# Column norms of three batches: squares summed in fp32 on the vector engine, norms from N=1 matmuls, down projection one step later

## The chip, the cores and the metric

The kernel runs on one core of a Trainium2 chip. A core has a matrix engine (TensorE, PE in the profile, with its weight loads as PEld), a vector engine (VectorE, DVE), a scalar engine (ScalarE, ACT), GpSimd (POOL) and SyncE (SP); the last two issue transfers here. The metric is the device time of one execution in microseconds. The kernel before takes 527.6 us, the median of 3 runs (527.09 to 528.2).

## The reference

Two layers follow each other, over 4 batches of 6208 rows and 256 columns, all in float32. The first is a cross-covariance attention: q and k are normalized **by column**, so each of their 256 columns needs the sum of its squares over all 6208 rows.

```python
qn = q / (np.linalg.norm(q, axis=1, keepdims=True) + 1e-06)
kn = k / (np.linalg.norm(k, axis=1, keepdims=True) + 1e-06)
s = kn.transpose(0, 2, 1) @ qn / tau          # 256 x 256 per batch
a = softmax(s, -1)
x = v @ a
```

The second is a channel mix with a gate (d_model 256, d_ff 1024), on x and x shifted by one row:

```python
xk = mu_k * x + (1.0 - mu_k) * x_prev
xr = mu_r * x + (1.0 - mu_r) * x_prev
k = np.maximum(xk @ w_k, 0.0)
out = sigmoid(xr @ w_r) * (k * k @ w_v)
```

## The kernel before

**Two kinds of work, interleaved.** The rows of a batch are cut in 12 blocks of 512 rows and a rest of 64 (`NB` is 12, `NBLK` is 49: 48 blocks and one more that takes the four rests). The second layer runs over the blocks. The covariance of batch b+1 has to be ready when the second layer comes to batch b+1; so batch 0's covariance is computed first, by itself, and those of batches 1 to 3 are computed in small pieces between the matmuls of the second layer.

**Covariance in groups and units.** A batch of q and k is loaded in 13 groups: one of 64 rows, and 12 that give each of the 128 partitions four rows. For batches 1 to 3 GpSimd loads and casts to bf16 (`group_load`, L106). A *unit* is one row per partition. Per unit the kernel issues two matmuls into `s_ps` (`unit_matmul`, L138, the matmul is L149), and per two units one square on ScalarE into `qk2` (`unit_square`, L130, the square is L136).

**Norms.** When a group's four units are through, `group_norms` (L158) adds its squares into `ssq_ps`: four matmuls with a 128x32 block of ones as weights and 512 squares as the moving operand, each in its own 32 columns of the array (L166). At the batch's end ScalarE copies `ssq_ps` out (L193), VectorE copies `s_ps` (L229), and `gather` turns the sums into a column per partition with four fp32 matmuls of one column (L202; the profile shows two passes of each). Batch 0 does the same for its first groups, and for its last ones goes another way (`norms_direct`, L172): the squares are the weights, a single column of ones is the moving operand, N=1, and the sum lands in `bank` directly (L179).

**Softmax in pieces.** `softmax_pieces` (L182) returns 16 short steps for batches 1 to 3: root, inverse, spreading the norms over columns, scaling, exponential, weighing. One is taken from the list `chain` at each step of the loop.

**The loop sets the order.** The schedule is manual: each engine executes what the program issues in the order in which it is written. The outer loop (L574) runs i from -2 to 47, the inner j from 0 to 7. At step (i, j) the program issues

- `finish` (L431) at even j: on ScalarE a tanh of the gate (L436), on VectorE `res` (L437), the product with the down projection. `vr_ps`, which both read, has two buffers;
- a piece of `chain`;
- `up(i+1, j)` (L392): two matmuls into `kT_ps` (L398, three buffers) and a Relu on ScalarE (L402); `square` of the step before on VectorE (L408);
- `down(i, j)` (L411): for even j the gate's two matmuls (L423) and three of the down projection (L427), for odd j the other five;
- for block i+2: at j = 0 and 2 `x_half` (L315: two matmuls, L327, and a copy on ScalarE, L329), at j = 3 to 5 and 7 `mix_delta` and `mix` (L373, L383) on VectorE, and at j = 1 a last `mix` for block i+1;
- a unit where j is in `slots`: six steps of eight for blocks 2 to 7, three to five for the next three, four for the others.

## Time and profile before

| | |
|---|---|
| median of 3 runs | 527.6 us |
| the profiled execution | 527.0 us |
| its span, first to last instruction | 525.2 us |
| busy: PE, DVE, ACT | 507.9, 404.6, 425.9 us |
| granted TensorE clock, mean | 0.999 |
| instructions | 10152 |

The span is what the profile covers; the execution's time has some 1.8 us around it. A line of the timeline gives the start and the length in us, then engine, line, operation, output and inputs with the program's names, and a count where like instructions are merged; in brackets stands idle time before it and what ended it. Matmuls are pipelined, so a line's length is longer than the time until the next can start; what a matmul costs is read from start to start. A line of the groups gives busy time and the mean length in ns, then idle time ahead of the group and what ended most of it. A row of the stretches gives start and end, the length, the busy time of PE, PEld, DVE, ACT and POOL with counts, the granted clock, the share of the DMA engines and GB/s.

### The profile page before, as it was taken

What the parts mean: (1) busy time and instruction counts of PE and PEld (TensorE: products, weight loads), DVE (VectorE), ACT (ScalarE), POOL (GpSimd) and SP (SyncE); (2) the same over time, 40 slices, a digit from 0 to 9 for tenths busy, and PEclk for the clock granted to TensorE, in tenths of its full rate; (3) what the DMA queues carried; (4) which work ended last, traced back from release to release, by engine and by line L of the source; (5) the groups of instructions that cost most, each with busy time, mean ns of one, the idle gap of its engine ahead of it and who ended that gap; (6) DMA issues with size and microseconds to landing.
All of it is one profiled execution on the core that took longest, in us unless ns stands there. A gap on an engine that the chain in (4) does not pass through costs nothing.

```text
span 525.2 us, 10152 instructions
## 1 busy us (share of the span) xinstructions
PE 507.9 (97%) x3656; PEld 335.4 (64%) x3656; DVE 404.6 (77%) x959; ACT 425.9 (81%) x814; POOL 101.9 (19%) x143
## 2 busy tenths in 40 slices
PE   4878999999999999999999999999999999999996
PEld 2454566666666666666666666666666666666665
DVE  4558766776788787777777877777889989898984
ACT  6885988889888888888878888878878777778774
POOL 0055142322332221211143131210030101000000
PEclk9999999999999999999999999999999999999999
DMA  8999999999999999989899999995278575424113
GB/s 329 420 287 194 178 179 211 199 150 175 167 190 171 145 181 160 164 120 150 133 158 199 152 148 188 153 143 118 61 125 141 102 158 111 115 76 105 59 64 100
DMA packets 143738, 83.76 MB, mean 159 GB/s; under 512 B 51716, under 2 KB 140104, under 8 KB 143688
## 3 DMA queue, kind: packets, MB, share of 16 engines
q0 software_dynamic: 65808, 33.01, 54.1%
q1 hardware_dynamic: 77712, 49.98, 40.9%
q8 instruction: 28, 0.46, 0.4%
q14 instruction: 22, 0.18, 0.1%
q10 hardware_dynamic: 168, 0.13, 0.1%
HBM read 78.71 MB, written 25.43 MB: 198 GB/s over the span
## 4 chain that ended last, share of the span: by engine, by line
PE 90%; DMA 5%; DVE 2%; ACT 1%; SPq 1%; issue 0%; DVEq 0%; ACTq 0%
PE kT_ps L398 32%; PE vr_ps L427 32%; PE vr_ps L423 8%; PE xT_ps L327 8%; PE s_ps L149 6%; PE ssq_ps L166 2%; DMA f_385<-in_k_dram 2%; DMA f_261<-in_k_dram 2%; DMA f_165<-in_k_dram 1%; SPq L115 1%; DVE xk L383 1%; PE bank L202 0%; PE bank L226 0%; PE y_ps L464 0%; ACT L209 0%
## 5 line engine op out<-in xcount | busy, mean ns | idle before, releaser
L402 ACT ACTIVATE kr<-kT_ps 128x512 bf16<-128x512 f32 (+1 forms) x392 | 230.5, 599 | 58.4 <-PE kT_ps L398 46.1
L398 PE MATMUL kT_ps<-xk,w_k_sb 128*128 128x512 bf16 (+1 forms) x784 | 231.4, 377 | 0.3 <-DVE xk L383 0.2
L427 PE MATMUL vr_ps<-w_v_sb,kk 128*128 128x256 bf16 x1536 | 230.5, 273 | 0.0
L427 PEld LDWEIGHTS <-kk 128*128 128x128 bf16 x1536 | 150.3, 98 | 58.0
L408 DVE TENSOR_TENSOR kk<-kr 128x512 bf16<-128x512 bf16 (+1 forms) x392 | 155.7, 417 | 4.8 <-ACT kr L402 4.1
L437 DVE SCALAR_TENSOR_TENSOR res<-res,vr_ps 128x256 f32<-128x256 f32 x192 | 80.5, 419 | 81.9 <-ACT res L436 79.6
L398 PEld LDWEIGHTS <-w_k_sb 128*128 128x128 bf16 x784 | 73.2, 98 | 36.1 <-DVE kk L408 4.8
L149 PE MATMUL s_ps<-qk 128*128 128x256 bf16 (+1 forms) x392 | 71.6, 282 | 6.1 <-DVE qk L126 6.1
L436 ACT ACTIVATE res<-vr_ps 128x256 f32<-128x256 f32 x192 | 74.7, 389 | 0.5
L329 ACT CAST xT<-xT_ps 128x512 bf16<-128x512 f32 x94 | 55.9, 594 | 22.9 <-PE xT_ps L327 22.8
L423 PE MATMUL vr_ps<-w_r_sb,xr 128*128 128x256 bf16 x384 | 73.3, 273 | 0.6 <-DVE xr L383 0.6
L383 DVE SCALAR_TENSOR_TENSOR xr<-delta,mu_t,xT 128x512 bf16<-128x512 bf16 x96 | 71.7, 747 | 0.0
L383 DVE SCALAR_TENSOR_TENSOR xk<-delta,mu_t,xT 128x512 bf16<-128x512 bf16 x96 | 71.6, 747 | 0.0
L423 PEld LDWEIGHTS <-xr 128*128 128x128 bf16 x384 | 37.5, 98 | 45.4 <-DVE xr L383 1.1
L120 POOL DMA_DIRECT2D qk<-in_q_dram x39 | 28.7, 737 | 183.2 <-ACT res L436 151.2
L327 PE MATMUL xT_ps<-vT,a_sb 128*128 128x512 bf16 x188 | 55.9, 379 | 0.0
L290 POOL DMA_DIRECT2D v_bf<-in_v_dram x48 | 37.1, 774 | 67.4 <-DMA vT<-v_bf 62.1
L149 PEld LDWEIGHTS <-qk 128*128 128x128 bf16 (+1 forms) x392 | 37.9, 101 | 18.0 <-DVE qk L126 9.0
L373 DVE TENSOR_TENSOR delta<-xT 128x1024 bf16<-128x1024 bf16 x48 | 33.1, 690 | 9.5 <-ACT xT L329 9.4
L120 POOL DMA_DIRECT2D qk<-in_k_dram x39 | 28.3, 726 | 2.8 <-DMA w_v_sb<-in_moe_w_v_dram 1.6
L327 PEld LDWEIGHTS <-a_sb 128*128 128x128 bf16 x188 | 18.4, 98 | 2.9 <-issue 0.6
L214 POOL TENSOR_TENSOR rn<-rn,half 128x4 f32<-128x4 f32 x3 | 3.1, 1036 | 55.4 <-DVE rn L211 55.4
(225 smaller groups left out, 234.6 us busy)
## 6 DMA issues: line engine op xcount, KB each, us to landing
out_dram<-res SPq DMA_DIRECT2D x47, 512.0 KB, 5.0
v_bf<-in_v_dram POOLq DMA_DIRECT2D x48, 256.0 KB, 9.2
qk<-in_q_dram POOLq DMA_DIRECT2D x36, 256.0 KB, 6.0
qk<-in_k_dram POOLq DMA_DIRECT2D x36, 256.0 KB, 8.1
vT<-v_bf SPq DMA_TRANSPOSE x45, 8.5
f_104<-in_q_dram SPq DMA_DIRECT2D x1, 512.0 KB, 3.4
f_106<-in_k_dram SPq DMA_DIRECT2D x1, 512.0 KB, 4.1
f_128<-in_q_dram SPq DMA_DIRECT2D x1, 512.0 KB, 5.4
```

Source lines behind the costliest of these rows:

```text
L120: nc.gpsimd.dma_start(qk[:rows, :n, i, :], qk_src(t, b, g))
L149: nc.tensor.matmul(s_ps[:, ih, :], qk[:rows, s, 1, ih * P:(ih + 1) * P], qk[:rows, s, 0, :], start=t0 and ih == 0, stop=te, skip_group_che ...
L327: nc.tensor.matmul(xT_ps, a_sb[:, b, ih, dh * P:(dh + 1) * P], vT[:, :, ih, :], start=ih == 0, stop=ih == 1)
L329: nc.scalar.copy(xT[:, dh, 1:], xT_ps)
L383: nc.vector.scalar_tensor_tensor(o[:, dh], st[i, "d"][:, dh], mu[:, dh:dh + 1], st[i, "x"][:, dh, :M], op0=OP.mult, op1=OP.add)
L398: nc.tensor.matmul(kT_ps[:, :m], w_k_sb[:, dh, fh * P:(fh + 1) * P], xk[:, dh, :m], start=dh == 0, stop=dh == 1)
L402: nc.scalar.activation(kr[:, :m], kT_ps[:, :m], AF.Relu, scale=0.5 ** 0.5)
L408: nc.vector.tensor_tensor(st[i, "kk"][:, fh, :m], kr[:, :m], kr[:, :m], op=OP.mult)
L423: nc.tensor.matmul(vr_ps[:, D:], xr[:, dh, s * P:(s + 1) * P], w_r_sb[:, dh, :], start=dh == 0, stop=dh == 1)
L427: nc.tensor.matmul(vr_ps[:, :D], kk[:, fh, s * P:(s + 1) * P], w_v_sb[:, fh, :], start=fh == 0, stop=fh == 7)
L436: nc.scalar.activation(res[:, s], vr_ps[:, D:], AF.Tanh, scale=0.5)
L437: nc.vector.scalar_tensor_tensor(res[:, s], res[:, s], 1.0, vr_ps[:, :D], op0=OP.add, op1=OP.mult)
```

## The change

For batches 1 to 3:

- a unit's square is written in fp32 instead of bf16, into `sq2`, in the space of batch 0's fp32 loads;
- VectorE adds up a group's four rows of squares: `first` adds rows 0 and 1 to rows 2 and 3 (128x1024), `second` the two halves of that (128x512), with bf16 out;
- `group_norms_at` takes that sum as weights: four matmuls of N=1 into `bank`, in place of the four of N=512 and the later gather. A group of one row per partition goes without additions;
- the additions are issued at steps j = 7, 0 and 1 (at a batch's end also at others, two at a time), the norms some steps later. The softmax pieces wait at the root until the batch's norms have been issued;
- the copy of `s_ps` goes to ScalarE, and the copy of `ssq_ps` is gone.

For the second layer, in all batches: `down(i, j)` is issued at step j+1 (the last of a block at the next block's step 0), `finish` at odd steps instead of even ones, and both halves of `xr` are mixed in the block before their use, at j = 0 and 2.

```diff
@@ unit_square
-            nc.scalar.activation(qk2[:rows, s:e], qk[:rows, s:e], AF.Square)
+            if n == 1:
+                t = pq.tile([P, 1, 2 * C], BF16, name="sq", tag="sq1", bufs=1)
+            else:
+                t = pq.tile([P, 2, 2 * C], F32, name="sq2", tag=f"f{s // 2}", bufs=6)
+            groups[b, g] += (t,)
+            nc.scalar.activation(t[:rows], groups[b, g][0][:rows, s:e].rearrange("p s i c -> p s (i c)"), AF.Square)
+            if e == n:
+                adds.extend((now[0] + 2, b, g, f) for f in (group_adds(b, g) if n == S else []))
+                norms.append((b, g))
+                ready[b, g] = now[0] + 2
+
+    def group_adds(b, g):
+        sq2 = groups[b, g][1:]
+        sq = pq.tile([P, 1, 2 * C], BF16, name="sq", tag="sq", bufs=4)
+        def first():
+            nc.vector.tensor_tensor(sq2[0], sq2[0], sq2[1], op=OP.add)
+            groups[b, g] = (groups[b, g][0], sq)
+        def second():
+            nc.vector.tensor_tensor(sq, sq2[0][:, 0:1], sq2[0][:, 1:2], op=OP.add)
+        return [first, second]
+
+    def group_norms_at(b, g):
+        rows, n = rows_of(b, g)
+        t = groups[b, g][1]
+        if b not in bank:
+            bank[b] = ps.tile([P, 2 * C], F32, name="bank", tag="ssq_ps")
+        for u in range(1 if n == 1 else 1):
+            for i in range(4):
+                nc.tensor.matmul(bank[b][:, C + i:C + i + 1], t[:rows, u, i * P:(i + 1) * P], ones[:rows, 0:1],
+                                 start=g == 0 and i == 0, stop=g == NB, skip_group_check=True)
...
@@ softmax_pieces
-            (nc.vector.tensor_copy if b else nc.scalar.copy)(s_sb, s_ps)
+            nc.scalar.copy(s_sb, s_ps)
...
-        return [both, None, gather, roots, roots2, None, invert, None, None, spread, None, scale,
+        return [evac, None, None, roots, roots2, None, invert, None, None, spread, None, scale,
                 None if bounded else top, exp, None, weigh]
...
@@ last_block
+        down(i - 1, 7)
...
@@ the loop
-            if j % 2 == 0:
-                if j == 0 and i >= 1:
+            if j % 2:
+                if j == 1 and i >= 1:
                     finish(i - 1, 3)
-                elif j > 0 and i >= 0:
+                elif j > 1 and i >= 0:
                     finish(i, j // 2 - 1)
...
-                piece = chain.pop(0)
+                piece = chain[0]
+                if len(chain) == ROOTS and any(e[0] == holds[0] for e in norms):
+                    piece = None
+                else:
+                    chain.pop(0)
...
-            if i >= 0:
-                down(i, j)
+            if j > 0 and i >= 0:
+                down(i, j - 1)
+            elif j == 0 and i >= 1:
+                down(i - 1, 7)
...
-                if j == 7 and n != 1:
-                    mix(n, "xr", 0)
-            if j == 1 and 0 <= i + 1 < NBLK:
-                mix(i + 1, "xr", 1)
-            if i == 0 and j == 6:
-                mix(1, "xr", 0)
+
+            if j in (0, 2) and 0 <= i + 1 < NBLK:
+                mix(i + 1, "xr", int(j > 0))
...
+            if adds and adds[0][0] <= now[0] and (j in (0, 1, 7) or adds[0][1] == holds[0] and chain and j in (1, 5, 7)):
+                for _ in range(2):
+                    _, *e, f = adds.pop(0)
+                    f()
+                    ready[tuple(e)] = now[0] + 2
+                    if not (adds and adds[0][1] == holds[0] and chain):
+                        break
+
+            if norms and ready[norms[0]] <= now[0] and not any(e[1:3] == norms[0] for e in adds) and (
+                    norms[0][0] == holds[0] or len(chain) < 4):
+                group_norms_at(*norms.pop(0))
+            now[0] += 1
```

The order of the instructions at three places. First PE in the steady stage, around one group's norms. Before, they follow the last unit of their own group (L149):

```order
L149 LDWEIGHTS qk
L149 MATMUL s_ps<-qk 128x256
L166 LDWEIGHTS ones
L166 MATMUL ssq_ps<-qk_2524,ones 32x512
L166 LDWEIGHTS ones
L166 MATMUL ssq_ps<-qk_2524,ones 32x512
L166 LDWEIGHTS ones
L166 MATMUL ssq_ps<-qk_2524,ones 32x512
L166 LDWEIGHTS ones
L166 MATMUL ssq_ps<-qk_2524,ones 32x512
L398 LDWEIGHTS w_k_sb
L398 MATMUL kT_ps<-xk,w_k_sb 128x512
```

Now (L355 is the old L327, L426 the old L398):

```order
L355 LDWEIGHTS a_sb
L355 MATMUL xT_ps<-vT,a_sb 128x512
L173 LDWEIGHTS sq
L173 MATMUL bank<-ones,sq 128x1
L173 LDWEIGHTS sq
L173 MATMUL bank<-ones,sq 128x1
L173 LDWEIGHTS sq
L173 MATMUL bank<-ones,sq 128x1
L173 LDWEIGHTS sq
L173 MATMUL bank<-ones,sq 128x1
L426 LDWEIGHTS w_k_sb
L426 MATMUL kT_ps<-xk,w_k_sb 128x512
```

The norms stand at the end of step j = 2, behind x_half, and wait for VectorE's `second`, issued two steps before. Second, DVE in the steady stage, from one `res` to the next but one. Before:

```order
L437 SCALAR_TENSOR_TENSOR res<-res,vr_ps 128x256
L408 TENSOR_TENSOR kk<-kr 128x512
L322 COPY xT<-xT 128x2
L408 TENSOR_TENSOR kk<-kr 128x512
L383 SCALAR_TENSOR_TENSOR xr<-delta,mu_t,xT 128x512
L437 SCALAR_TENSOR_TENSOR res<-res,vr_ps 128x256
```

Now, in steps j = 7 and 0 (L465 is the old L437, L436 the old L408, L411 the old L383):

```order
L465 SCALAR_TENSOR_TENSOR res<-res,vr_ps 128x256
L436 TENSOR_TENSOR kk<-kr 128x512
L158 TENSOR_TENSOR sq_3392<-sq_3392,sq_3465 128x1024
L436 TENSOR_TENSOR kk<-kr 128x512
L350 COPY xT<-xT 128x2
L411 SCALAR_TENSOR_TENSOR xr<-delta,mu_t,xT 128x512
L162 TENSOR_TENSOR sq<-sq_3392 128x512
L465 SCALAR_TENSOR_TENSOR res<-res,vr_ps 128x256
```

Both additions of a group stand between two `res`. Third, DVE at the end of batch 1 (steps j = 7 of block 7 and j = 0 of block 8), where the copy of `s_ps` stood before:

```order
L437 SCALAR_TENSOR_TENSOR res<-res,vr_ps 128x256
L229 COPY s_sb<-s_ps 128x512
L408 TENSOR_TENSOR kk<-kr 128x512
L322 COPY xT<-xT 128x2
L408 TENSOR_TENSOR kk<-kr 128x512
L383 SCALAR_TENSOR_TENSOR xr<-delta,mu_t,xT 128x512
L437 SCALAR_TENSOR_TENSOR res<-res,vr_ps 128x256
```

Now:

```order
L465 SCALAR_TENSOR_TENSOR res<-res,vr_ps 128x256
L436 TENSOR_TENSOR kk<-kr 128x512
L158 TENSOR_TENSOR sq_1677<-sq_1677,sq_1721 128x1024
L162 TENSOR_TENSOR sq<-sq_1677 128x512
L436 TENSOR_TENSOR kk<-kr 128x512
L350 COPY xT<-xT 128x2
L411 SCALAR_TENSOR_TENSOR xr<-delta,mu_t,xT 128x512
L158 TENSOR_TENSOR sq_1792<-sq_1792,sq_1840 128x1024
L162 TENSOR_TENSOR sq<-sq_1792 128x512
L465 SCALAR_TENSOR_TENSOR res<-res,vr_ps 128x256
```

The additions of the batch's last two groups stand together between two `res`.

More of the change, by code (lines that the diff above doesn't have):

```diff
@@ L84 @@
     cov = {}
+    bank = {}
+    adds = []
+    norms = []
+    ready = {}
+    now = [0]
     groups = {}
@@ L151, in unit_matmul @@
                              skip_group_check=True)
-        if s == n - 1 and not late:
-            if b == 0 and g > DIRECT:
+        if s == n - 1 and b == 0:
+            if g > DIRECT:
                 norms_direct(g)
@@ L167, in group_norms @@
                              qk2[:rows, u].rearrange("p i c -> p (i c)"),
-                             start=(b, u) not in summed, stop=g == (len(sizes(b)) - 1 if b else DIRECT), tile_position=(0, 32 * u),
+                             start=u not in summed, stop=g == DIRECT, tile_position=(0, 32 * u),
                              skip_group_check=True)
-            summed.add((b, u))
+            summed.add(u)
     def norms_direct(g):
@@ L178, in norms_direct @@
             for i in range(4):
-                nc.tensor.matmul(cov["bank"][:, C + i:C + i + 1], flat[:, i * P:(i + 1) * P], ones[:rows, 0:1],
+                nc.tensor.matmul(bank[0][:, C + i:C + i + 1], flat[:, i * P:(i + 1) * P], ones[:rows, 0:1],
                                  start=False, stop=g == len(sizes(0)) - 1 and u == n - 1, skip_group_check=True)
@@ L224, in spread @@
         def spread():
-            nc.tensor.matmul(cov[b][:, :C], ones_f, rq_d, start=True, stop=True)
+            nc.tensor.matmul(bank[b][:, :C], ones_f, rq_d, start=True, stop=True)
         def evac():
-            (nc.vector.tensor_copy if b else nc.scalar.copy)(s_sb, s_ps)
+            nc.scalar.copy(s_sb, s_ps)
         def scale():
-            nc.vector.tensor_tensor(s_sb, s_sb, cov.pop(b)[:, :C].unsqueeze(1).to_broadcast([P, 2, C]), op=OP.mult)
+            nc.vector.tensor_tensor(s_sb, s_sb, bank[b][:, :C].unsqueeze(1).to_broadcast([P, 2, C]), op=OP.mult)
         def top():
@@ L251, in halves @@
         def halves():
-            rq = cov.pop(b)[:, :C]
+            rq = bank[b][:, :C]
             for ih in range(2):
@@ L520 @@
     chain = []
-    waiting = []
+    ROOTS = 13
+    holds = [0]
     def unit(ahead=2):
@@ L529, in unit @@
         feed(max(ahead, 1))
-        busy = len(chain) > 2
-        unit_matmul(*u, late=busy)
-        if busy and u[2] == sizes(u[0])[u[1]] - 1:
-            waiting.append(u[:2])
+        unit_matmul(*u)
         pos["mm"] += 1
@@ L538, in unit @@
             chain.extend(softmax_pieces(u[0]))
+            holds[0] = u[0]
     def next_load():
```

49 lines of the change are left out of this document (16 added, 33 removed).

## The prediction, made before the changed kernel ran

> **What bounds the kernel now.** The first view is the page's busy time, with the span.
>
> ```profile
> span 525.2 us, 10152 instructions
> PE 507.9 (97%) x3656; PEld 335.4 (64%) x3656; DVE 404.6 (77%) x959; ACT 425.9 (81%) x814; POOL 101.9 (19%) x143
> ```
>
> PE's busy time is modelled, so 97% alone proves little. The second view is PE's timeline over one block in the steady stage, batch 2, where each block of the loop carries one covariance group. Columns: start, length, line and operation, count.
>
> ```profile
> 201.52 0.71 PE L427 MATMUL vr_ps<-w_v_sb,kk 128*128 128x256 bf16 x5
> 202.07 0.38 PE L149 MATMUL s_ps<-qk 128*128 128x256 bf16 x2
> 202.29 0.59 PE L398 MATMUL kT_ps<-xk,w_k_sb 128*128 128x512 bf16 x2
> 202.72 0.38 PE L423 MATMUL vr_ps<-w_r_sb,xr 128*128 128x256 bf16 x2
> 202.94 0.49 PE L427 MATMUL vr_ps<-w_v_sb,kk 128*128 128x256 bf16 x3
> 203.26 0.59 PE L327 MATMUL xT_ps<-vT,a_sb 128*128 128x512 bf16 x2
> 203.70 0.59 PE L398 MATMUL kT_ps<-xk,w_k_sb 128*128 128x512 bf16 x2
> ...
> 209.02 0.38 PE L149 MATMUL s_ps<-qk 128*128 128x256 bf16 x2
> 209.33 0.40 PE L166 MATMUL ssq_ps<-qk_2381,ones 128*32 128x512 bf16 x4
> 209.66 0.61 PE L398 MATMUL kT_ps<-xk,w_k_sb 128*128 128x512 bf16 x2
> ...
> 211.52 0.71 PE L427 MATMUL vr_ps<-w_v_sb,kk 128*128 128x256 bf16 x5
> ```
>
> Read the starts, not the lengths. Five L427 take 0.55 us from start to start (0.11 each), a pair of L398 0.43, a pair of L149 0.22, gate plus three L427 0.54, a pair of L327 0.44, and no row names an idle time. Each start follows the one before by what its own matmuls need, and the block takes 211.52 - 201.52 = 10.00 us: here PE's stream sets the time. The only irregular place is 209.02 to 209.66, where the norms stand. The engine that receives work is DVE, so its reserve is the third view: its busy time in one steady stretch, and in the stretch in which batch 2's softmax ends.
>
> ```profile
> 205.00:215.00 10.00, 10.00 (x74) 6.68 (x72) 7.71 (x19) 8.31 (x18) 2.23 (x3) 1.00 1.08 158
> 275.00:285.00 10.00, 10.00 (x74) 6.29 (x73) 9.03 (x23) 8.74 (x20) 2.70 (x4) 1.00 1.30 218
> ```
>
> After the stretch stand PE, PEld, DVE, ACT, POOL. DVE works 7.71 us in a steady block of 10.00 and has 2.29 free; the second stretch leaves 0.97. The granted clock is 1.00.
>
> **The change, part by part.** *Removed from PE.* From L149 over the four L166 to L398 is 209.66 - 209.02 = 0.64 us, without them 202.29 - 202.07 = 0.22: a group's norms cost 0.42 us. 36 groups: 15.1 us. The three one-row groups and the three gathers of the column sums:
>
> ```profile
> 276.79 0.38 PE L149 MATMUL s_ps<-qk 128*128 128x256 bf16 x2
> 277.10 0.39 PE L166 MATMUL ssq_ps<-qk_3243,ones 64*32 64x512 bf16 x1
> 277.42 0.60 PE L398 MATMUL kT_ps<-xk,w_k_sb 128*128 128x512 bf16 x2
> ...
> 261.61 0.75 PE L427 MATMUL vr_ps<-w_v_sb,kk 128*128 128x256 bf16 x5
> 262.19 0.95 PE L202 MATMUL bank<-thirty_83,ssq 128*128 128x1 f32 x8
> 263.01 0.59 PE L398 MATMUL kT_ps<-xk,w_k_sb 128*128 128x512 bf16 x2
> ```
>
> The one-row group costs 0.63 - 0.22 = 0.41, three 1.2 us. The gather costs 263.01 - 261.61 = 1.40 less the 0.55 of its five L427: 0.85, three 2.6 us. Removed in all: 18.9 us.
>
> *Added on PE.* 39 sets of four N=1 matmuls. Batch 0 has the same form:
>
> ```profile
> 33.26 0.54 PE L179 MATMUL bank<-ones,qk_336 128*128 128x1 bf16 x16
> 33.66 1.03 PE L149 MATMUL s_ps<-qk 128*128 128x256 bf16 x8
> ...
> 35.37 0.34 PE L179 MATMUL bank<-ones,qk_419 128*128 128x1 bf16 x8
> 35.60 0.61 PE L149 MATMUL s_ps<-qk 128*128 128x256 bf16 x4
> ```
>
> Sixteen take 0.40 us and eight 0.23, so four lie between 0.10 (a quarter of sixteen) and 0.23 (no less than eight); I take 0.13, near the line through both. 39 x 0.13 = 5.1. PE's net is 18.9 - 5.1 = 13.8 us less (9.9 to 14.9 by the bounds). A steady block becomes 10.00 - 0.42 + 0.13 = 9.71.
>
> One rule speaks against the size of this. The Trainium skill, page "TensorE: Matmul & The Clock Gate", section "Part 3: Packing small matmuls", says that matmuls in different column tiles run together, in the time of one plus some 4 ns each; with its back-to-back gap of 216 ns for N=512 a group would cost an estimated 0.23 us, and the whole saving would be 7 us instead of 13.8. The trace agrees that the four start together, but the 0.42 us between neighbours is measured, so I go by the row.
>
> *Added on DVE.* Per group one fp32 add of 128x1024 and one of 128x512. The nearest rows, and DVE's pitch when it runs without a gap:
>
> ```profile
> L437 DVE SCALAR_TENSOR_TENSOR res<-res,vr_ps 128x256 f32<-128x256 f32 x192 | 80.5, 419 | 81.9 <-ACT res L436 79.6
> L232 DVE TENSOR_TENSOR s_sb<-s_sb,bank 128x512 f32<-128x512 f32 x3 | 2.0, 681 | 0.0
> ...
> 203.63 0.42 DVE L437 SCALAR_TENSOR_TENSOR res<-res,vr_ps 128x256 f32<-128x256 f32 x1 [1.59 <-ACT res L436]
> 203.97 0.75 DVE L408 TENSOR_TENSOR kk<-kr 128x512 bf16<-128x512 bf16 x2
> 204.64 0.69 DVE L373 TENSOR_TENSOR delta<-xT 128x1024 bf16<-128x1024 bf16 x1
> 205.37 0.42 DVE L437 SCALAR_TENSOR_TENSOR res<-res,vr_ps 128x256 f32<-128x256 f32 x1
> 205.70 0.42 DVE L408 TENSOR_TENSOR kk<-kr 128x512 bf16<-128x512 bf16 x1
> 206.04 0.75 DVE L383 SCALAR_TENSOR_TENSOR xk<-delta,mu_t,xT 128x512 bf16<-128x512 bf16 x1
> 206.70 0.42 DVE L408 TENSOR_TENSOR kk<-kr 128x512 bf16<-128x512 bf16 x1
> ```
>
> Two-input fp32 work takes 419 ns at 256 and 681 at 512: 262 per 256 more, so 1,205 at 1024. The next instruction starts about 0.08 before the end (0.42 to 0.34, 0.75 to 0.66): 1.12 + 0.60 = 1.72 us per group. Below, if fp32 ran as fast as the bf16 delta (690 for 1024): 0.94. Above, twice L232 and once L232 without overlap: 2.04. Both rows are the same kind of work, so I take 1.72. The Trainium skill, "VectorE: DVE Perf Modes", section "The perf-mode tier table", keeps fp32 tensor_tensor at one element a cycle; its formula gives an estimated 1.22 and 0.69 us, and the sum stays.
>
> A steady block then needs 7.71 + 1.72 = 9.43 us of DVE against PE's 9.71: covered, with 0.28 to spare. It is not covered in three places.
> - Batch 1. Its units stand six to a block, 1.5 groups; two blocks there run from 84.99 to 106.28:
>
> ```profile
> 84.99 0.59 PE L327 MATMUL xT_ps<-vT,a_sb 128*128 128x512 bf16 x2
> 106.28 0.59 PE L327 MATMUL xT_ps<-vT,a_sb 128*128 128x512 bf16 x2
> ```
>
>  10.65 us each. PE comes to 10.65 - 1.5 x 0.29 = 10.21, DVE to 7.71 + 1.5 x 1.72 = 10.29: 0.08 over, six blocks, 0.5 us.
> - Batch 1's end. The order shows two groups' adds (3.44 us) between a res and the next. With res, two squares, xr, that is 0.34 + 0.67 + 0.66 + 3.44, with the small copy 5.2 us, in two steps that take PE 0.43 x 2 + 0.55 + 0.54 + 0.22 + 0.44 = 2.61. DVE starts there about 1.2 us into the step (203.63 - 202.29 = 1.34 now), ends at 6.4; the norms that need the last sum stand at the end of the second step after, 2.61 + 2.5 = 5.1. PE waits about 1.3 us, once.
> - The ends of the batch 1 and batch 2 softmaxes: 9.03 + 1.72 = 10.75 in a stretch that PE could do in 9.2 (two groups and a one-row group: 10.00 - 1.25 + 0.39). A late res holds the gate matmul two steps later, for there are two vr_ps buffers, and two steps are 2.6 us; after tanh and res themselves about half of that is reserve. Most of 1.6 us is absorbed: I take 0.5 each, 1.0.
>
> Together 2.8 us are given back.
>
> *At nothing.* The squares on ACT now write fp32 of the same size, and ACT copies s_ps where it copied ssq; by the row below fp32 out costs no more than L402's bf16 of the same size, and L136's 1,052 ns stays.
>
> ```profile
> L193 ACT COPY ssq<-ssq_ps 128x512 f32<-128x512 f32 x3 | 1.8, 587 | 0.2 <-PE ssq_ps L166 0.2
> L402 ACT ACTIVATE kr<-kT_ps 128x512 bf16<-128x512 f32 (+1 forms) x392 | 230.5, 599 | 58.4 <-PE kT_ps L398 46.1
> 62.92 0.39 PE L423 MATMUL vr_ps<-w_r_sb,xr 128*128 128x256 bf16 x2 [0.57 <-DVE xr L383]
> out_dram<-res SPq DMA_DIRECT2D x47, 512.0 KB, 5.0
> ```
>
> Without that cover 75 squares would cost ACT their difference, and ACT has 1.7 us a block free. The output's issue on SP comes one step later; it lands in 5.0 us and three res buffers last 30. No load moves on POOL. The down projection one step later moves no matmul out of the program: 0.54 us leaves the start and stands at the end. Block 1's xr is mixed six steps earlier, which can remove the 0.57 us wait; against that 0.54 less work stands there, so 0.
>
> **Sum.** 527.0 (the profiled execution; span 525.2) - 13.8 + 2.8 = 516.0. The median of the runs is 0.6 above that execution: 516.6.
>
> **The rivals.**
> - *DVE paces the loop, mildly.* DVE executes in order and waits for tanh 79.6 us now, 1.66 a block. If some of it stays though DVE is late, the block is 9.43 plus what stays. At 0.43 us the steady block is 9.86: 24 x 0.15 = 3.6, and batch 1 6 x 0.51 - 0.5 = 2.6, so 522.8. For it: 0.28 is a thin reserve. Against: a late DVE finds tanh done.
> - *Slower: the ring res, gate, tanh, res closes.* DVE late holds vr_ps, PE's gate waits, tanh follows it, DVE idles again. Half of today's wait, 0.8, gives 24 x 0.52 + 6 x 0.88 - 0.5 = 17.3 more: 533.9. It decides from 0.59 us a block on, where 24(x - 0.28) + 6(x + 0.08) - 0.5 reaches the 11 gained. Against: two steps of reserve, and finish moved behind the even step's matmuls, ahead of the ACT square that delayed tanh to 1.59 above.
> - *The removed norms were cheap*, because a neighbour hides their gap: 0.23 a group instead of 0.42, 36 x 0.19 = 6.8 less, 523.4. (The Trainium skill's page named above would have it so.) Against: 0.64 against 0.22.
> - *PE does not bind*, and removing its work gives nothing: 527.6. The Trainium skill, "Trainium Kernel Development and Optimization", section "Performance Expectations", calls matmul busy a bad metric and LDWEIGHTS busy a good one. PEld is 64%. Against: the starts fill 10.00 us.
>
> **How the numbers follow.** Forecast 0.58, its own range 513.5 to 519.5; mild pacing 0.22; slower 0.12; cheap norms 0.04; PE not binding 0.04. A measurement here tells 0.2%, about 1 us, from nothing. Faster: 0.58 + 0.04 and nearly all of 0.22: 0.83. Same 0.05, slower 0.12. The range runs from 513 (nothing given back, 513.8, and part of the early wait) to 524.5, past the mild case; outside lie the slower case, PE not binding and some edge.
>
> **What would show it.** Steady blocks of 9.7 us between L427 groups, four N=1 matmuls in 0.13; adds near 1.20 and 0.68 us; DVE busy near 9.4 of 9.7, its wait for tanh far under 79.6; PE waiting once near the end of batch 1, about 1.3 us, for a DVE sum. Wrong would be steady blocks of 9.9 or more with PE waiting for res or sums, or adds over 2.0 us a group.

## The result, and the profile after

The changed kernel takes 515.82 us, the median of 4 runs (514.83 to 516.28), beside 527.9 us for the kernel before (527.09 to 528.2): the ratio is 0.9771, with a 95% interval of 0.9752 to 0.9791. Two later comparisons gave 516.34 us (0.9789, 0.9776 to 0.9803) and 515.57 us (0.9773, 0.9754 to 0.9792). The prediction said 516.6 us. The profiled execution took 514.83 us, 12.2 less than the one before.

The page's span and busy times of the changed kernel:

```profile
span 513.1 us, 10142 instructions
PE 491.3 (96%) x3580; PEld 336.7 (66%) x3641; DVE 457.8 (89%) x1028; ACT 424.7 (83%) x814; POOL 102.5 (20%) x143
```

DVE rose from 404.6 to 457.8 us in a shorter span. PE's timeline over a steady block of batch 2, the one that answers to the prediction's second fence (L455 is the old L427, L355 the old L327, L426 the old L398, L173 the new norms):

```profile
196.80 0.71 PE L455 MATMUL vr_ps<-w_v_sb,kk 128*128 128x256 bf16 x5
197.34 0.59 PE L355 MATMUL xT_ps<-vT,a_sb 128*128 128x512 bf16 x2
197.78 0.24 PE L173 MATMUL bank<-ones,sq 128*128 128x1 bf16 x4
197.88 0.59 PE L426 MATMUL kT_ps<-xk,w_k_sb 128*128 128x512 bf16 x2
...
206.45 0.71 PE L455 MATMUL vr_ps<-w_v_sb,kk 128*128 128x256 bf16 x5
```

The block is 206.45 - 196.80 = 9.65 us long (10.00 before), and four N=1 matmuls take 197.88 - 197.78 = 0.10 us from start to start. No row has an idle time. Now DVE, in a steady stretch and in batch 1's stage (after the length stand PE, PEld, DVE, ACT, POOL):

```profile
200.00:210.00 10.00, 9.95 (x74) 6.97 (x75) 9.59 (x22) 8.66 (x18) 2.24 (x3) 1.00 1.06 158
75.00:125.00 50.00, 49.68 (x380) 35.09 (x385) 49.96 (x106) 44.91 (x85) 13.77 (x19) 1.00 1.40 193
```

From the groups, a first add and `res`, and from DVE's timeline a second add:

```profile
L158 DVE TENSOR_TENSOR sq_1677<-sq_1677,sq_1721 128x1024 f32<-128x1024 f32 x1 | 1.2, 1220 | 0.0
L465 DVE SCALAR_TENSOR_TENSOR res<-res,vr_ps 128x256 f32<-128x256 f32 x192 | 80.1, 417 | 28.6 <-ACT res L464 27.9
```

```profile
137.63 0.69 DVE L162 TENSOR_TENSOR sq<-sq_1792 128x512 bf16<-128x512 f32 x1
```

In the steady stage DVE works 9.59 of 10.00 us, which is 9.25 of a block's 9.65: 0.40 is free. In batch 1's stage it has 0.04 us free in 50. Its wait for tanh fell from 79.6 to 27.9 us.

Between 60 and 390 us PE waits at two places only, as its timeline shows them:

```profile
136.81 0.59 PE L355 MATMUL xT_ps<-vT,a_sb 128*128 128x512 bf16 x2
138.38 0.25 PE L173 MATMUL bank<-ones,sq 128*128 128x1 bf16 x4 [0.96 <-DVE sq L162]
...
388.82 0.65 PE L355 MATMUL xT_ps<-vT,a_sb 128*128 128x512 bf16 x2 [0.38 <-DVE a_sb L280]
```

At the end of batch 1 the last group's norms wait for its sum: 1.57 us from the pair before instead of 0.44, 1.13 lost. At the end of batch 3's softmax the first `x_half` of the next batch waits for the weighted matrix `a_sb`.

For the account over the whole loop: `x_half` stands on PE at step 0 of each i. Its starts cut the execution into stretches of the same work. For the changed kernel three such rows, at i = 1, 11 and 45:

```profile
63.19 0.59 PE L355 MATMUL xT_ps<-vT,a_sb 128*128 128x512 bf16 x2
165.77 0.59 PE L355 MATMUL xT_ps<-vT,a_sb 128*128 128x512 bf16 x2
484.51 0.59 PE L355 MATMUL xT_ps<-vT,a_sb 128*128 128x512 bf16 x2
```

The table gives differences of such starts in us (165.77 - 63.19 = 102.58 is the changed kernel's second row), and beside the two kernels five of the experiments below.

| stretch | before | changed | shift alone | no shift | no sums | adds after | both ends |
|---|---|---|---|---|---|---|---|
| start to i = 1 | 63.47 | 63.19 | 62.47 | 63.50 | 64.80 | 64.42 | 63.54 |
| i = 1 to 10, batch 1 and its end | 107.21 | 102.58 | 107.15 | 107.09 | 105.28 | 104.92 | 102.40 |
| 11 to 19, batch 2 | 90.06 | 87.03 | 90.07 | 91.61 | 89.73 | 87.04 | 87.03 |
| 20 to 22, its end | 32.12 | 30.20 | 32.07 | 32.86 | 31.02 | 30.41 | 30.41 |
| 23 to 31, batch 3 | 90.06 | 87.04 | 90.06 | 91.60 | 89.74 | 87.03 | 87.04 |
| 32 to 34, its end | 27.31 | 27.51 | 28.06 | 27.10 | 27.38 | 26.61 | 26.61 |
| 35 to 44 | 86.96 | 86.96 | 86.95 | 86.96 | 86.96 | 86.95 | 86.95 |
| i = 45 to the end | 28.0 | 28.5 | 28.5 | 28.0 | 28.5 | 28.0 | 28.0 |

The change gains 4.6 + 3.0 + 1.9 + 3.0 us where groups are normed, loses 0.2 at batch 3's end, and 0.5 behind the loop, where the last down projection now stands.

### The profile page after: what moved, and what is told of

The parts are those of the page before. It is cut to its first block, busy times and chain, and to the rows that moved or that the text cites. A ratio compares the mean times of both kernels' runs of the same rounds, so it can differ in the third digit from the quotient of the medians.

```text
span 513.1 us, 10142 instructions
## 1 busy us (share of the span) xinstructions
PE 491.3 (96%) x3580; PEld 336.7 (66%) x3641; DVE 457.8 (89%) x1028; ACT 424.7 (83%) x814; POOL 102.5 (20%) x143
## 5 line engine op out<-in xcount | busy, mean ns | idle before, releaser
L430 ACT ACTIVATE kr<-kT_ps 128x512 bf16<-128x512 f32 (+1 forms) x392 | 234.0, 600 | 48.4 <-PE kT_ps L426 30.5
L455 PE MATMUL vr_ps<-w_v_sb,kk 128*128 128x256 bf16 x1536 | 230.2, 273 | 0.4
L426 PE MATMUL kT_ps<-xk,w_k_sb 128*128 128x512 bf16 (+1 forms) x726 | 218.6, 376 | 1.3 <-DVE xk L411 0.2
L455 PEld LDWEIGHTS <-kk 128*128 128x128 bf16 x1536 | 150.2, 98 | 57.6 <-issue 0.4
L436 DVE TENSOR_TENSOR kk<-kr 128x512 bf16<-128x512 bf16 (+1 forms) x392 | 157.8, 415 | 1.0 <-ACT kr L430 0.9
L465 DVE SCALAR_TENSOR_TENSOR res<-res,vr_ps 128x256 f32<-128x256 f32 x192 | 80.1, 417 | 28.6 <-ACT res L464 27.9
L426 PEld LDWEIGHTS <-w_k_sb 128*128 128x128 bf16 x784 | 73.3, 98 | 23.4 <-issue 1.0
L187 PE MATMUL s_ps<-qk 128*128 128x256 bf16 (+1 forms) x392 | 73.1, 288 | 5.8 <-DVE qk L132 5.8
L411 DVE SCALAR_TENSOR_TENSOR xr<-delta,mu_t,xT 128x512 bf16<-128x512 bf16 x96 | 71.6, 746 | 0.0
L411 DVE SCALAR_TENSOR_TENSOR xk<-delta,mu_t,xT 128x512 bf16<-128x512 bf16 x96 | 71.4, 745 | 0.0
L451 PEld LDWEIGHTS <-xr 128*128 128x128 bf16 x384 | 37.5, 98 | 44.9 <-issue 0.7
L355 PE MATMUL xT_ps<-vT,a_sb 128*128 128x512 bf16 x188 | 56.0, 379 | 0.9 <-DVE vT L338 0.6
L355 PEld LDWEIGHTS <-a_sb 128*128 128x128 bf16 x188 | 18.4, 98 | 4.7 <-issue 1.5
```

The costliest lines, as they stand in the source:

```text
L187: nc.tensor.matmul(s_ps[:, ih, :], qk[:rows, s, 1, ih * P:(ih + 1) * P], qk[:rows, s, 0, :], start=t0 and ih == 0, stop=te, skip_group_che ...
L355: nc.tensor.matmul(xT_ps, a_sb[:, b, ih, dh * P:(dh + 1) * P], vT[:, :, ih, :], start=ih == 0, stop=ih == 1)
L411: nc.vector.scalar_tensor_tensor(o[:, dh], st[i, "d"][:, dh], mu[:, dh:dh + 1], st[i, "x"][:, dh, :M], op0=OP.mult, op1=OP.add)
L426: nc.tensor.matmul(kT_ps[:, :m], w_k_sb[:, dh, fh * P:(fh + 1) * P], xk[:, dh, :m], start=dh == 0, stop=dh == 1)
L430: nc.scalar.activation(kr[:, :m], kT_ps[:, :m], AF.Relu, scale=0.5 ** 0.5)
L436: nc.vector.tensor_tensor(st[i, "kk"][:, fh, :m], kr[:, :m], kr[:, :m], op=OP.mult)
```

## The experiments

**Shift alone.** The kernel before with only the order of the second layer changed.

```diff
-            if i >= 0:
-                down(i, j)
+            if j > 0 and i >= 0:
+                down(i, j - 1)
+            elif j == 0 and i >= 1:
+                down(i - 1, 7)
```

and `finish` and the mixes of xr moved as in the change.

> The kernel before with only the order changed: down projection one step later, finish on odd steps, xr mixed where the change mixes it; squares and norms as before. My theory (PE sets the time, a shift removes no matmul from it): steady block 10.00 us as before, the 0.57 us wait for xr at the start gone, down's 0.54 us standing at the end instead: 527.9 us within 1 us, ratio 0.998 to 1.002. Rival (part of the 12 us came from the shift, because vr_ps is freed earlier): steady block 9.9 or less, 525 us or less.

527.96 us; ratio 1.0011 (0.9999 to 1.0023), steady block 9.99 to 10.00. As the theory had it, the shift by itself is worth nothing. But the table's row of batch 3's end grows from 27.31 to 28.06, with no add in the program. What is late there is `a_sb` (L248):

```profile
400.20 0.42 DVE L437 SCALAR_TENSOR_TENSOR res<-res,vr_ps 128x256 f32<-128x256 f32 x1
400.53 0.16 DVE L246 RECIPROCAL sm<-sm 128x2 f32<-128x2 f32 x1
400.73 0.61 DVE L248 TENSOR_SCALAR a_sb<-s_sb,sm 128x256 bf16<-128x256 f32 x2
```

With `finish` on odd steps a `res` stands ahead of the weighing, in the last step before the next batch needs it. So that loss belongs to the shift and not to the sums. And the tail grows by 0.5.

**No shift.** The changed kernel with `down`, `finish` and xr at their old places: the first experiment's edit, backwards.

> The changed kernel without the shift: down, finish and xr stand where they stood before; sums on VectorE and N=1 norms stay. Theory A (the shift is what gives VectorE's res the reserve that the two adds eat): with two vr_ps buffers a late res holds the gate matmul, PE waits for res, steady block 9.8 to 10.1 us, 519 to 526 us. Rival B (VectorE's free 0.4 us a block is enough wherever res stands): steady block 9.65, 515 to 517 us. The end of batch 3's softmax, where the shift put weigh behind a res (0.88 us lost), should lose less than that under both.

531.47 us; ratio 1.0071 (1.0052 to 1.0091): slower than the kernel before, outside both forecasts, and some 16 us above the changed kernel. The steady block is 10.16. The longest row of PE's waits between 60 and 390 us (us in all, times, the longest):

```profile
PE vr_ps L455 <- DVE kk L436: 11.3, 27, 1.1
```

The one such place of a steady block, on PE's timeline and on DVE's:

```profile
212.11 0.60 PE L455 MATMUL vr_ps<-w_v_sb,kk 128*128 128x256 bf16 x4
213.05 0.28 PE L455 MATMUL vr_ps<-w_v_sb,kk 128*128 128x256 bf16 x1 [0.33 <-DVE kk L436]
```

```profile
211.11 1.22 DVE L158 TENSOR_TENSOR sq<-sq,sq 128x1024 f32<-128x1024 f32 x1
212.24 0.41 DVE L465 SCALAR_TENSOR_TENSOR res<-res,vr_ps 128x256 f32<-128x256 f32 x1
212.57 0.42 DVE L436 TENSOR_TENSOR kk<-kr 128x512 bf16<-128x512 bf16 x1
```

The fifth matmul of a run of five starts 0.94 us after the first instead of 0.44: these 0.50 are the whole loss of a block (10.16 - 9.65 = 0.51). It reads the last kk of the block, which `square(i, 7)` writes at step 0 and the down projection of step 1 needs. The add of step 7 stands on DVE ahead of it. Theory A had the right effect and the wrong tile: PE waits for kk, and no row of its waits names `res`. The reserve could have been read from the kernel before, on DVE's timeline in the block of the prediction's second fence:

```profile
200.41 0.42 DVE L408 TENSOR_TENSOR kk<-kr 128x512 bf16<-128x512 bf16 x1
```

That kk is done at 200.83, and the fifth of the five L427 that start at 201.52 needs it at 201.52 + 4 x 0.11 = 201.96: 1.13 us of reserve, all of which an add of 1.13 takes. In the run that kk came another 0.44 us too late (212.57 + 0.42 = 212.99 instead of 212.11 + 0.44 = 212.55), and that is what PE waits for. These 0.44 are PE's own gain. Before, a group's norms stood between the five matmuls of step 7 and those of step 1; in the run they stand elsewhere. The rows before, and the one of the run:

```profile
198.48 0.71 PE L427 MATMUL vr_ps<-w_v_sb,kk 128*128 128x256 bf16 x5
199.34 0.40 PE L166 MATMUL ssq_ps<-qk_2271,ones 128*32 128x512 bf16 x4
```

```profile
209.51 0.71 PE L455 MATMUL vr_ps<-w_v_sb,kk 128*128 128x256 bf16 x5
```

From five to five PE took 201.52 - 198.48 = 3.04 us before and 212.11 - 209.51 = 2.60 now, while the last kk starts 1.93 us behind the first of these five before and 3.06 now, later by the add's 1.13 and nothing else. So the change itself cuts the reserve from 1.13 to 0.69 us.

**No sums.** The changed kernel without the additions: squares in bf16, sixteen N=1 matmuls per group.

```diff
-                t = pq.tile([P, 2, 2 * C], F32, name="sq2", tag=f"f{s // 2}", bufs=6)
+                t = pq.tile([P, 2, 2 * C], BF16, name="sq2", tag=f"f{s // 2}", bufs=6)
-                adds.extend((now[0] + 2, b, g, f) for f in (group_adds(b, g) if n == S else []))
...
-        for u in range(1 if n == 1 else 1):
+        for u in range(n):
```

> The changed kernel without the sums: ACT writes the squares in bf16 as before, VectorE adds nothing, and each group's norms are 16 N=1 matmuls instead of 4. Theory (the price is the norm matmuls' own, 0.10 us per four, 0.40 per sixteen): steady block 9.65 + 0.30 = 9.95 us; 36 x 0.30 = 10.8 us more than the changed kernel, less the 1.1 us wait at batch 1's end and 0.4 of batch 1's VectorE-bound blocks, so 525 us, and VectorE 1.72 us a block less busy. Rival (the norms' form gave the gain, how many N=1 matmuls hardly matters because a neighbour hides them): steady block 9.65 to 9.75, 514 to 518 us.

525.58 us; ratio 0.996 (0.9946 to 0.9973). Around a steady group (L186 is the unit, L172 the norms, L425 the up projection):

```profile
203.97 0.38 PE L186 MATMUL s_ps<-qk 128*128 128x256 bf16 x2
204.18 0.54 PE L172 MATMUL bank<-ones,sq 128*128 128x1 bf16 x16
204.59 0.59 PE L425 MATMUL kT_ps<-xk,w_k_sb 128*128 128x512 bf16 x2
```

Sixteen take 0.41 us, as much as the four N=512 of the old form (0.42), and the steady block is 9.96. So the N=1 form alone gains next to nothing in the steady stage. What gains is that the sums on DVE turn sixteen into four. The rival falls: no neighbour hides N=1 matmuls. What is left of the gain are the one-row groups and the gathers, less the shift's loss at batch 3's end.

**More work for DVE.** How large the reserve is, and what happens behind it:

```diff
+            if j == 6 and (12 <= i < 20 or 24 <= i < 32):
+                for _ in range((i // 4 - 2) if i < 20 else (i // 4 - 3)):
+                    nc.vector.tensor_tensor(idle, fill, fill, op=OP.mult)
```

> The changed kernel with extra VectorE work whose result is not used: bf16 multiplications 128x512 (0.335 us from start to start) late in step 6, one a block in blocks 12 to 15, two in 16 to 19, three in 24 to 27, four in 28 to 31. Theory (reserve 9.65 - 9.25 = 0.40 us a block, beyond it VectorE alone paces): 9.65, 9.92, 10.26, 10.59 us a block. Rival 1 (a late res closes the ring over vr_ps and tanh): beyond the reserve a block grows by more than VectorE's own excess, two doses at 10.2 or more. Rival 2 (VectorE still idles for tanh, so it is bound before 0.40): one dose already above 9.75. Rival 3 (the gaps between VectorE's instructions hold more reserve): 9.65 at two doses too.

522.3 us in a single run. One multiplication a block: four blocks of 9.65, nothing lost. Two: 9.66, 9.66, 9.87, 9.73, and then 10.54 in the block behind them, where the changed kernel has 9.66, 9.66, 9.78, 9.65, 9.65. The five together lose 1.06 us, and 4 x (0.67 - 0.40) is 1.08: it is paid in full, but two blocks late. Three: 10.32 a block once the lateness is used up; the last of those blocks as a stretch:

```profile
322.75:333.07 10.32, 9.83 (x74) 6.66 (x72) 10.25 (x24) 8.41 (x17) 2.70 (x4) 1.00 1.10 160
```

DVE works 10.25 of 10.32, and 9.25 + 3 x 0.335 is 10.26. So a DVE over its reserve of 0.40 paces the loop one for one at three, with 0.07 a block on top: rivals 1 and 2 fall there, and rival 3 holds for two blocks only. With four it is not as clean: blocks of 10.66 to 10.90 stand against 9.25 + 4 x 0.335 = 10.59. The blocks with three and four, and the three behind them, into which batch 3's end falls, lose 7.4 us together, where DVE's excess is 4 x 0.605 + 4 x 0.94 = 6.2; the remaining 1.2 is not explained by the excess, so a ring that costs something at four is not excluded.

**Spread.** For the two waits of the changed kernel: another place for an add before batch 1's end, and weigh one step earlier.

```diff
-                None if bounded else top, exp, None, weigh]
+                None if bounded else top, exp, weigh]
...
-    ROOTS = 13
+    ROOTS = 12
...
-  (j in (0, 1, 7) or adds[0][1] == holds[0] and chain and j in (1, 5, 7)):
+  (j in (0, 1, 7) or j == 6 and 6 <= i < 8 and len(adds) > 2 or adds[0][1] == holds[0] and chain and j in (1, 5, 7)):
```

> The changed kernel with two places taken out where PE waits for VectorE: batch 1's last two groups are summed one add at a time (step 6 of blocks 6 and 7 is a further place for an add) instead of two groups' adds in a row, and the empty step between exp and weigh of the softmax is dropped, so that weigh comes a step earlier. My theory: the 1.1 us wait at batch 1's end goes and of the 0.9 us at the end of batch 3's softmax at least half: 515.8 - 1.1 - 0.5 to 0.9 = 513.8 to 514.2 us. Rival (both are only symptoms of VectorE's backlog, which is paid wherever the adds stand): 515.3 to 516.3.

516.91 us; ratio 0.9798 (0.9785 to 0.9812): no better than the changed kernel (0.9771 to 0.9789). Two rows tell why:

```profile
138.85 0.25 PE L173 MATMUL bank<-ones,sq 128*128 128x1 bf16 x4 [0.83 <-DVE sq L162]
...
152.75 0.25 PE L173 MATMUL bank<-ones,sq 64*128 64x1 bf16 x4 [0.82 <-DVE s_sb L264]
```

The adds came a step earlier, the norms with them, and PE waits for the sum as before. The second wait is new and was made by this edit: with one piece fewer in the list the next batch's first norms are let go a step too soon, while the scaling still reads their bank. It stands at the ends of batches 1 and 2, and costs 0.9 each time. The earlier weigh itself helped: the block at batch 3's end took 9.45 instead of 9.83 to 10.00.

**Adds after.** No shift, and the adds in steps where they stand behind the last kk:

```diff
-  (j in (0, 1, 7) or adds[0][1] == holds[0] and chain and j in (1, 5, 7)):
+  (j in (0, 1, 2) or adds[0][1] == holds[0] and chain and j in (1, 3, 5)):
```

> The changed kernel without the shift, as in the run without it, but the adds stand in steps 0, 1 and 2 instead of 7, 0 and 1 (1, 3, 5 instead of 1, 5, 7 at a batch's end). In step 0 an add stands behind the square of the last kk on VectorE, in step 7 ahead of it. Theory after that run: what the shift buys is only time for that last kk, which the first down projection of a block needs in the same step and which stood behind the 1.13 us add; so here the steady block is 9.65 to 9.7 us, the end of batch 3's softmax loses nothing (9.1 instead of 10.0), down's 0.54 us is back at the start: 514 to 517 us. Rival (a res ahead of down's matmuls, the vr_ps ring, is what holds PE without the shift): steady block still 10.0 or more, 525 us or more.

517.24 us; ratio 0.9805 (0.9791 to 0.9818), steady block 9.66, batch 3's end 9.11. DVE's timeline, to be compared with the run without shift, and the five matmuls on PE's:

```profile
207.83 0.41 DVE L465 SCALAR_TENSOR_TENSOR res<-res,vr_ps 128x256 f32<-128x256 f32 x1
208.16 0.42 DVE L436 TENSOR_TENSOR kk<-kr 128x512 bf16<-128x512 bf16 x1
...
208.56 1.22 DVE L158 TENSOR_TENSOR sq<-sq,sq 128x1024 f32<-128x1024 f32 x1
```

```profile
208.84 0.71 PE L455 MATMUL vr_ps<-w_v_sb,kk 128*128 128x256 bf16 x5
```

The last kk is done at 208.58, 0.7 us before its matmul, which is the reserve of 0.69 worked out above, and PE doesn't wait. So it was the place of one add, not the old order of `res`, that cost 0.5 a block; the shift gives that kk a step more time, and moving the add does the same. What this run loses against the changed kernel stands at batch 1's end (104.92 instead of 102.58), where the norms come a step later than before and with them the weighing. There PE waits 1.28 us for the last group's sum, 0.39 for a kk, and 1.14 for `a_sb`:

```profile
159.41 0.65 PE L355 MATMUL xT_ps<-vT,a_sb 128*128 128x512 bf16 x2 [1.14 <-DVE a_sb L280]
```

**The changed kernel again**, beside the last two.

> The changed kernel once more, beside the others on the same chip: 515.8 us as before (514.8 to 516.5). Its first x_half starts later or earlier than in the kernel before by as much as the loads' arrivals vary: if the 1.4 us that it was late in the first profile belongs to the change, it is there again; if it is chance, it lies between -0.5 and 1.4.

516.34 us. Its first `x_half` started at 46.10, between the two kernels' (45.35 and 46.75). The first profile had a granted clock of 0.50 from 34.1 to 37.5 us, where the second and the kernel before had 1.00. The four profiles with such a stretch before the first `x_half` come to it at 45.82 to 46.75, the ten without at 45.29 to 46.10; so the clock can account for a part of the 1.4 us, and the change is not shown to have a share in it. But at i = 1 it met a wait that the first profile had not:

```profile
65.76 0.59 PE L355 MATMUL xT_ps<-vT,a_sb 128*128 128x512 bf16 x2 [2.27 <-DMA vT<-v_bf]
```

**Norms later.** The changed kernel with the last group's norms of batch 1 a step later, weigh a step earlier, and the gate of the next batch's norms mended.

```diff
-                    ready[tuple(e)] = now[0] + 2
+                    ready[tuple(e)] = now[0] + (3 if tuple(e) == (1, NB) else 2)
...
-                    norms[0][0] == holds[0] or len(chain) < 4):
+                    norms[0][0] == holds[0] or len(chain) < 3):
```

> The changed kernel with the norms of batch 1's last group one step later (adds where they are), weigh a step earlier in the softmax's order as in the spread run, and the next batch's norms held until two pieces are left instead of three, so that they don't meet the scale that still reads their bank. My theory (PE waits for a sum because the order lets it arrive 1.1 us after the point where PE needs it; a step is 1.2 us): the wait at batch 1's end goes, block 10 falls from 10.88 to about 9.9 us, blocks 11 and 23 stay at 10.6, the end of batch 3's softmax falls from 9.8 to 9.45: 1.4 us less than the changed kernel on the same chip. Rival (VectorE's backlog there is paid by some other PE wait if not by this one): block 10 or the two after it lose what is won, within 0.4 us of the changed kernel.

515.08 us; ratio 0.9767 (0.975 to 0.9785), beside 0.9773 for the changed kernel in the same comparison: not told apart. The expectation counts blocks from the first `x_half`; its blocks 10, 11 and 23 are i = 8, 9 and 21. They took 10.77, 10.60 and 10.60, and batch 3's end 9.45 as forecast. (This profile's block i = 1 took 11.54 instead of 9.87, for its granted clock was 0.50 from 65.1 to 68.5 us; the edit changes nothing there.) The wait for the sum is gone, and another is there in its place:

```profile
141.40 0.38 PE L451 MATMUL vr_ps<-w_r_sb,xr 128*128 128x256 bf16 x2 [0.86 <-DVE res L465]
```

Here the rival is right: DVE is behind at that place, and PE waits for whatever DVE writes next. It is also the one wait for vr_ps that a row shows.

**Both ends.** The same without the shift, with the adds behind the last kk.

```diff
+  (j in (0, 1, 2) or 6 <= i < 8 and j == 5 or adds[0][1] == holds[0] and chain and j in (1, 5)):
```

> As the run just described, without the shift, the adds in steps 0, 1 and 2 (and 5 in blocks 6 and 7; 1 and 5 at a batch's end). If the shift buys nothing but time for the last kk, this has the steady block of 9.65, no loss at the end of batch 3's softmax (9.1 instead of 9.45 us) and no wait at batch 1's end: 0.3 us less than the run just described, 1.7 less than the changed kernel. Rival: as there; a wait for the weighted matrix or for a kk at batch 1's end shows that the order without the shift has less room: 1 us more than the changed kernel.

514.4 us; ratio 0.9756 (0.9737 to 0.9774). The table's last column: batch 3's end is 26.61 instead of 27.51 and the tail 28.0 instead of 28.5. At batch 1's end 0.34 and 0.36 us of waits are left, and the stretch takes 102.40; at batch 2's end 0.2 is lost (30.41 instead of 30.20). So it is 1.2 us less than the changed kernel of the same comparison (below), where 1.7 was expected.

**The changed kernel a third time**, in the same comparison.

> The changed kernel once more for the comparison on one chip: ratio to the kernel before 0.977 to 0.979, 515.5 to 516.5 us.

515.57 us; ratio 0.9773 (0.9754 to 0.9792). At i = 1 it waits again:

```profile
64.10 0.59 PE L355 MATMUL xT_ps<-vT,a_sb 128*128 128x512 bf16 x2 [1.94 <-DMA vT<-v_bf]
```

**Half of the sum left out.** What batch 1's stage costs if DVE has less to do, and all else stands where it is:

```diff
-            nc.vector.tensor_tensor(sq2[0], sq2[0], sq2[1], op=OP.add)
+            if b > 1:
+                nc.vector.tensor_tensor(sq2[0], sq2[0], sq2[1], op=OP.add)
```

> The changed kernel with the first add of batch 1's groups left out (the 128x1024 one; those norms then count two of the four rows): VectorE has 12 x 1.13 us less to do in blocks 2 to 9, everything else stands where it stood. Theory now (VectorE is full in batch 1's stage, and the wait at its end is that backlog coming due): the wait for a sum at batch 1's end goes, block 10 falls from 10.88 to about 9.7 us, and from the third to the thirteenth x_half it takes about 101.3 us instead of 102.6. Rival (the order of norms and adds at the end makes the wait, whatever VectorE did before): block 10 stays above 10.5 us. A second rival (nothing of batch 1's loss is VectorE's): 102.4 or more.

513.98 us in a single run. The block i = 8 takes 9.75 us instead of 10.88, and no wait of PE is left at batch 1's end. The block i = 2 takes 10.09 instead of 10.36. The blocks i = 3 to 7 stay what they were: 10.19, 10.10, 10.19, 10.22, 10.20, beside 10.20, 10.09, 10.19, 10.22, 10.20 in the changed kernel. So those were PE's own, though DVE was full in them there. From i = 1 to 10 it takes 101.17 us, 1.41 less than with all adds: DVE's overload in batch 1 costs 1.4 us, 1.1 of it in one piece at the end and 0.3 in the block i = 2.

**Both ends again**, on another occasion.

> The kernel without the shift, with the adds in steps 0 to 2 and weigh a step earlier, once more: 514 to 515 us, ratio to the kernel before 0.975 to 0.977. If its lead of 1.2 us over the changed kernel in the last comparison was chance, 515.5 or more.

514.33 us; ratio 0.9764 (0.9738 to 0.979). With the run above that is twice 514.4 beside 515.8, 516.3 and 515.6 for the changed kernel. The intervals of the ratios overlap, so the times alone don't separate the two. The traces do: from i = 1 to 44 it takes 420.44 and 420.84 us against 421.32, 421.15 and 421.15, and the tail is 0.5 shorter. About 1 us is gained, mostly at the two places where the shift costs something.

## Why the prediction was right, and where it was not

**What bounds the kernel** was read rightly. PE's stream sets the time; removing PE work shortened every steady block by what the rows said. That rival (PE doesn't bind) is out; so are the cheap norms: a steady block gained 0.34 us, and with removed norms of 0.23 it would have gained 0.13. The Trainium skill's "Trainium Kernel Development and Optimization", section "Performance Expectations", has LDWEIGHTS busy as a good metric for how close a kernel is to roofline. PEld's share went from 64 to 66%; what showed that PE binds were its starts. The Trainium skill's span rule ("TensorE: Matmul & The Clock Gate", "Part 3: Packing small matmuls"), by which they would cost an estimated 0.23, does not give the cost of these four matmuls between their neighbours; the measured 0.42 decides.

**The added N=1 matmuls** were taken at 0.13 us per four and measured 0.10, the lower bound: 39 x 0.03 = 1.2 us too little gain. The extrapolation had put a fixed cost in the line through eight and sixteen that four do not have. (The Trainium skill, "TensorE: Matmul & The Clock Gate", "Wait — 56ns, not 53.3ns?", has a floor of about 25 ns from start to start however small N is, which gives an estimated 0.10; the trace agrees, 26 ns, and the sum would have been better by it.) Removed less added is then 18.9 - 3.9 = 15.0 instead of 13.8 (the prediction's bound of 14.9 is the same sum, a tenth off).

**The adds** were 1,220 and 690 ns at the rows shown, against 1,205 and 681. (The formula of the Trainium skill's "VectorE: DVE Perf Modes", section "The TRN2 errata", gives an estimated 1.22 and 0.69; the trace agrees.) The steady block was 9.65 against 9.71, DVE 9.25 against 9.43. The reserve was 0.40 and not 0.28, since DVE needed 0.18 less than summed and PE 0.06 less, and the experiment with more work puts it at 0.40 too. The chance for mild pacing had its mechanism right in part: over the reserve DVE sets the block, 10.32 for 10.26 of work, with 0.07 left over where 0.43 was taken.

**Batch 1** was costed as 0.5 in its blocks and 1.3 at its end. The end wait came at the predicted place and size, 1.13 us. The 0.5 did not come block by block: but for 0.3 in the block i = 2 the blocks stayed PE's 10.2, DVE fell behind in them and the end paid. Together 1.4 instead of 1.8, by the run with half the sum left out. The prediction named two losses where there is one: a backlog, and the place where it comes due. Moving that place (spread, norms later) moved the wait and saved 0.1 at most.

**The ends of the softmaxes** were costed at 0.5 each, for lateness of `res`. At batch 2's end the stretch without sums takes 31.02; with three groups at 0.30 less it would be 30.12, and it took 30.20: 0.1 was lost. Batch 3's end lost 0.9 (0.7 in the two later profiles), where nothing was forecast, and there the shift is the cause: it puts a `res` ahead of the weighing.

**The sum.** 15.0 - 1.4 - 0.1 - 0.9 = 12.6, beside 12.4 measured from i = 1 to 44; the tail costs 0.5, and the start gave 0.3. The forecast's 13.8 - 2.8 = 11.0 was near because a gain that it took too small (the N=1 matmuls cost less than it said) stood against losses that were too large, and one that it lacked. The mechanism was right; that the sum came within 0.8 us is in part luck.

**The step that failed** is "the down projection one step later moves no matmul out of the program: so 0". Alone it is 0, as forecast. But the adds stand in steps 7 and 0, and with the old places of the second layer this kernel is slower than the one before by 0.7%. The slower rival asked the right question, where a late DVE holds PE, and looked for it at `res` and vr_ps. The nearest deadline was another: the last kk, needed 1.13 us after it is written, and 0.69 once the old norms are gone from between. Had the prediction gone through all that stands behind the new add on DVE, with each product's own deadline, it would have found that the shift is what keeps the add off the path, and that another step for the add would do as well.

**At the start** the forecast was 0, and one profile says little about it. The shift takes down's 0.54 us out of the first block, but PE then waits 0.56 there for a transposed tile (`vT`, in the changed kernel and in the run with the shift alone), so that block gains nothing: 6.82 us with the shift, 6.64 in the three runs with the adds behind the last kk and no shift. (The 7.46 of the kernel before has a wait of 0.65 in its middle that those three do not have.) The block after it does gain, for the 0.57 us wait for xr is gone, as the prediction said it could be. So PE comes to the first `x_half` that uses a transposed load earlier than before: 16.4 us after the first `x_half`, instead of 18.1 (16.7 with the shift alone, its wait of 0.24 for the load left out). In the three profiles of the changed kernel it waited 0, 2.27 and 1.94 us there, and 0 in the one before. So part of what is gained up to there goes to that load. The first profile, without the wait, was the fastest of its four runs.

## What to carry to other kernels

Before work is put on an engine that executes in order, go through what stands behind it there and read for each product when it is needed: the smallest of these reserves counts, not the idle time of a block. Read them as they will be after the change: work taken away ahead of the reader brings the deadline nearer, here by 0.44 us. An edit that is worth nothing alone can be the cover without which its companion costs more than it brings, so undo each part of a change singly, and apply each singly. Where an engine is overfull for a stage, look for the loss at the stage's end, and expect a moved deadline to move the wait and not to remove it.

## What the runs showed of the hardware

Matmuls of N=1 with full weight loads took 26 ns each from start to start (sixteen in 0.41 us, four in 0.10). Sixteen of them cost as much as four of N=512 in 32 columns each, which start together (within 10 ns) and still put off the next full matmul by 0.42 us.

A DVE that is over its work for two blocks shows nothing in the block's length: some 0.5 us of lateness went by before PE felt it (9.66 and 9.66 under a load of 9.92), and afterwards nearly all of it was paid (1.06 of 1.08 us for four such blocks).

The transposed load for i = 1 lands at different times. SP's issues in the first and in the second profile of the changed kernel:

```profile
54.08 4.84 SPq L325 DMA_TRANSPOSE vT<-v_bf  x2
```

```profile
55.72 5.30 SPq L325 DMA_TRANSPOSE vT<-v_bf  x2
```

In the first PE starts at 63.19 without a wait, at most 9.1 us behind the first of the two issues; in the second at 65.76, 10.0 us behind it. So of the 2.57 us between these starts 1.64 come from a later issue and 0.93 from the way behind it. Where PE waited for this load, 9.0 to 10.5 us lay between issue and use. The profiles with the new norms show waits from 0 to 2.36 us at that one place, and what decides is not settled here. It makes a single profile's start a poor witness for differences of 2 us, so the comparisons above begin behind it.
